# Retention and feed-forward products of a mixed pair: interleaved, or each in one go

## The chip, the cores and the metric

The kernel runs on one core of one Trainium2 chip. The metric is the device time in microseconds of one execution; a kernel's time is the median over its runs. TensorE (PE) does the matrix products, VectorE (DVE) and ScalarE (ACT) the element-wise work, GpSimd (POOL) a little on the side, and SyncE's queue (SP) issues all transfers.

## The reference

```
ret  = (q kᵀ / 8) * D          per head; D[i,j] = gamma_h^(i-j) for i >= j, else 0
x    = ret @ v                 B=4, 8 heads, 576 positions, head size 64 -> 2304 tokens x 512
xn   = x / rms(x) * rms_g
y    = (silu(xn @ w_gate) * (xn @ w_val)) @ w_out        512 -> 1536 -> 512
out  = relu(y @ w_in)^2 @ w_out2                         512 -> 2048 -> 512
```

All inputs and outputs are float32.

## The kernel before, in words

**Retention.** Two heads make a pair (128 partitions); there are 16 pairs, and pair n is written n here, pieces of it `name(n)`. The 576 positions are cut in chunks of 128 (the last of 64). Four functions do a pair: `scores(n, half)` multiplies q and k of two or three chunks into bank pair A1 (half 0) or A0 (half 1), and DVE multiplies the result with the decay mask into `ret`; `state(n)` (L256) makes four 128x64 chunk states `u` from k and v in one PSUM bank, ACT copies the first one to `R[:, 0]` and DVE makes `R[:, 1]` to `R[:, 3]` from it one after the other (L269 and L271); `outputs(n, half)` (L277) adds `R` times q and `ret` times v in a bank of tag V, and DVE writes it to X (L298). Loop pass n does scores and state of pair n and outputs of pair n-1.

**Feed-forward.** A float32 product is three products of high and low parts (`mm3`, L386 to L388). A block `pg` or `pv` is twelve matmuls of 512 columns into a bank of tag G; ACT applies silu to `pg` (L426), DVE multiplies `pv` with it (L434). Tags G and V have two banks each, handed out in turn: a tile waits until the last reader of the tile two before it in its tag is through.

**Weights.** Each weight piece is loaded raw (512 KB, L101) to one of three buffers and converted by `convert_piece`: two ACT copies (L124, L125), three DVE steps (L126, L129, L132), an ACT copy to the high part (L137), a DVE subtraction for the low part (L138). The load of a piece waits until L132 has read the buffer of the piece three before it. `halves(k)` counts half pieces and converts when there are two. `CONVERT_BEHIND` says for a phase whether a conversion is issued behind the last ACT and DVE instruction then known ("ad") or may go ahead of them ("").

**Order.** PE and SP take their instructions in the order of the code. The order on ACT, DVE and POOL is set when the kernel is built, by a planner with its own estimate of times; each engine then takes its instructions strictly in that order. Passes 1 to 7 have retention alone. From pass 8 on ("mixed") `block()` at two points of a pass puts feed-forward blocks of the first 512 tokens between the retention products: ten gate and ten value blocks at 17 points up to pass 16. `NORMS` says in which pass and half the normalization steps of 256 tokens come (squares, roots, scale, split), and `LOAD_W` where one more weight piece is loaded ahead.

Of the kernel before, what the change touches and what calls it, by code (L numbers as in the profile page):

```python
# [25 lines left out]
NPAIR = B * HP  # L26
HALF = (2 * C, S - 2 * C)
NMAX = 512
T1 = [512, 256, 512, 512, 512]
# [5 lines left out]
ORDER = [*range(NBESIDE, NF1), *range(NBESIDE)]  # L35
NWA, NWC = NGV + NKEPT // 2, 1
NWB = NF1 - NKEPT // 2 - NWC
SKIP = 1
FIRST = 7
WARM = (8, 6, 5, 5)  # L40
WARM_PAIR = {1: (1, 1), 2: (1, 1)}
NORMS = {
    (4, 0): [("squares", 0)], (4, 1): [("squares", 1)], (5, 0): [("roots", 0)], (5, 1): [("roots", 1)],
    (6, 1): [("scale", 0), ("split", 0)], (7, 0): [("scale", 1), ("split", 1)],
    (9, 1): [("squares", 2)], (11, 0): [("roots", 2)], (12, 0): [("scale", 2)],
}
LOAD_W = (3,)
CONVERT_ALONE = {2: 2, 3: 2, 7: 2}
CONVERT_BEHIND = ("", "", "ad", "ad")
RSQRT_MAGIC = float(0x5F3759DF)  # L50
# [6 lines left out]
def retention_then_glu_then_relu2(ctx: ExitStack, tc: tile.TileContext, qk, kv, w1, w2, g, cmask, cvs, cgi, cgc, cid, out):  # L57
# [15 lines left out]
    def bank(tag, name):  # L73
        return psum.tile([P, 512], F32, tag=tag, name=name)
# [30 lines left out]
    def load_ahead(i):  # L105
        while cv["load"] < min(i + cv["ahead"], cv["load_lim"]):
            load_piece()

    def convert():
        i = cv["done"]  # L110
        if i not in raws or i >= cv["lim"]:
            return False
        raw = raws.pop(i)
        with ExitStack() as behind:
            for e in CONVERT_BEHIND[cv["phase"]]:
                behind.enter_context(tc.issue_after(last_on[e].ins))
            convert_piece(i, raw)
        cv["done"] += 1
        return True
# [21 lines left out]
    def halves(k):  # L141
        cv["half"] += k
        while cv["half"] >= 2 and convert():
            cv["half"] -= 2
        cv["half"] = min(cv["half"], 2)

    def need(n):
        while cv["done"] < n:
            assert convert()
# [9 lines left out]
    alone = {"on": True}  # L159
# [13 lines left out]
    def load_kv(n):  # L173
        if n >= NPAIR:
            return
        if n > 1:
            raw_k[n] = kvp.tile([P, 4, P], F32, tag="k", name=f"k{n}")
            vsc[n] = ap.tile([P, 5, P], F32, tag="v", name=f"v{n}", bufs=4)
        else:
            t = X[:, 2 + n, :9 * P].rearrange("p (c n) -> p c n", c=9)  # L180
            raw_k[n], vsc[n] = t[:, :4], t[:, 4:]
        nc.sync.dma_start(out=raw_k[n], in_=kv[n][:, :4])
        nc.sync.dma_start(out=vsc[n], in_=kv[n][:, 4:])
# [10 lines left out]
    def keep_warm(k, new=False):  # L194
        if new:
            junk["t"] = bank("G", f"junk{len(junk)}")
        for _ in range(k):
            nc.tensor.matmul(junk["t"][:, :P], zero, zero, start=True, stop=True)
# [36 lines left out]
    def scores(n, half):  # L235
        hp = n % HP
        ps = bank2("A0" if half else "A1", f"s{n}_{half}")
        for j in range(2 + half):
            w = REM if j == 2 else C
            for h in range(2):  # L240
                score(ps[:w, h, j * C:j * C + w], n, 2 * half + j, h, w)
        t = ap.tile([P, 2, 2 * C], F32, tag="ret", name=f"ret{n}_{half}", bufs=3)
        last_on["d"] = nc.vector.tensor_tensor(
            out=t.rearrange("p h (c i) -> p h c i", c=2),
            in0=ps[:, :, :2 * C].rearrange("p h (c i) -> p h c i", c=2),
            in1=mask[:, 2 * hp:2 * hp + 2, None, :].to_broadcast([P, 2, 2, C]),
            op=ALU.mult,
        )
        rets[n, half] = t
        if half:  # L250
            last_on["d"] = nc.vector.tensor_tensor(
                out=ret4[n % 2][:REM], in0=ps[:REM, :, 2 * C:2 * C + REM],
                in1=mask[:REM, 2 * hp:2 * hp + 2, :REM], op=ALU.mult,
            )

    def state(n):  # L256
        hp = n % HP
        u = bank("G" if alone["on"] else "V", f"u{n}")
        for c in range(4):
            for h in range(2):  # L260
                r = slice(h * D, h * D + D)
                nc.tensor.matmul(
                    u[r, c * D:c * D + D], raw_k[n][:, c, r], vsc[n][:, c, r],
                    start=True, stop=True,
                )
        if n > 1:
            load_kv(n + 2)
        R = ap.tile([P, 4, D], F32, tag="R", name=f"R{n}")
        last_on["a"] = nc.scalar.activation(out=R[:, 0], in_=u[:, 0:D], func=AF.Copy)  # L269
        for c in range(1, 4):  # L270
            last_on["d"] = nc.vector.scalar_tensor_tensor(  # L271
                out=R[:, c], in0=R[:, c - 1], scalar=gc[:, hp:hp + 1], in1=u[:, c * D:c * D + D],
                op0=ALU.mult, op1=ALU.add,
            )
        Rs[n] = R

    def outputs(n, half):  # L277
        b, hp = divmod(n, HP)
        po = bank("V", f"o{n}_{half}")
        ret = rets.pop((n, half))  # L280
        chunks = ((0, C), (1, C)) if half == 0 else ((2, C), (3, C), (4, REM))
        both = [slice(h * D, h * D + D) for h in range(2)]
        for c, w in chunks:
            o = (c - 2 * half) * C
            for r in both if c else ():
                nc.tensor.matmul(
                    po[r, o:o + w], Rs[n][r, c - 1], raw_qk[n][r, 0, c * C:c * C + w],
                    start=c == max(1, 2 * half), stop=False, skip_group_check=True,
                )
        for c, w in chunks:  # L290
            o = (c - 2 * half) * C
            for h, r in enumerate(both):
                rhs = ret4[n % 2][:, h] if c == 4 else ret[:, h, o:o + w]
                nc.tensor.matmul(
                    po[r, o:o + w], vsc[n][:, c, r], rhs, start=False, stop=c == chunks[-1][0], skip_group_check=True,
                )
        t0, w = b * S + half * 2 * C, HALF[half]
        last_on["d"] = nc.vector.tensor_tensor(out=X[:, hp, t0:t0 + w], in0=po[:, :w], in1=gi[:, hp, :w], op=ALU.mult)  # L298
        if half:
            load_qk(n + 4)  # L300
# [69 lines left out]
    def split_x(tok, n, col0=0):  # L370
        for k in range(KC):
            src_, d = X[:, k, tok:tok + n], slice(col0, col0 + n)
            last_on["a"] = nc.scalar.activation(out=xh[:, k, d], in_=src_, func=AF.Copy)
            last_on["d"] = nc.vector.tensor_tensor(out=xl[:, k, d], in0=src_, in1=xh[:, k, d].bitcast(F32), op=ALU.subtract)  # L374


    off1 = [sum(T1[:i]) for i in range(len(T1))]
# [96 lines left out]

    cv["lim"] = cv["load_lim"] = NGV
    blocks = [(kind, f) for f in range(NBESIDE) for kind in (glu_gate, glu_val)]
    NPOINT = 2 * (NPAIR - FIRST) - SKIP
    points = {"n": -SKIP, "done": 0}

    def block():  # L480
        points["n"] += 1
        while points["done"] < min(len(blocks), points["n"] * len(blocks) / NPOINT):
            i = points["done"]
            need(i + 1)
            blocks[i][0](0, blocks[i][1], "G")
            points["done"] += 1
            halves(1)

    def stages(n, half):
        with tc.high_priority():  # L490
            for what, i in NORMS.get((n, half), ()):
                beside(what, i)

    for n in range(1, NPAIR + 1):
        mixed = n > FIRST
        if n in LOAD_W:
            cv["ahead"] += 1
            load_ahead(cv["done"])
        if n == FIRST + 1:
            alone["on"] = False  # L500
            cv["phase"] = 2
        if n == FIRST + 2:
            cv["phase"] = 1
        if n < NPAIR:
            scores(n, 0)
        if mixed:
            block()
        else:
            keep_warm(WARM_PAIR.get(n, (0, 0))[0], n in WARM_PAIR)
        outputs(n - 1, 0)  # L510
        stages(n, 0)
        if n < NPAIR:
            state(n)
            if n == NPAIR - 1:
                att_kv.close()
                wpool["c"] = ctx.enter_context(tc.tile_pool(name="wc", bufs=NWC, side="right", reuse_waits="tile"))
                cv["lim"] = NGV + NWC
                cv["load_lim"] = NP1
                load_ahead(cv["done"])
        if mixed:  # L520
            block()
        else:
            keep_warm(WARM_PAIR.get(n, (0, 0))[1])
        if n < NPAIR:
            scores(n, 1)
        outputs(n - 1, 1)
        stages(n, 1)
        scale_v(n + 1)
        halves(CONVERT_ALONE[n] if n in CONVERT_ALONE else 2 * mixed)
    need(NGV)  # L530
    assert points["done"] == len(blocks)
    att.close()
# [10 lines left out]
    for f in range(NBESIDE, NF1):  # L543
# [2 lines left out]
        halves(1)  # L546
        glu_val(0, f, "G")
        halves(1)
    split_x(off1[1], T1[1])
    norms = iter(())  # L550
    LAG = 2
    for f in range(NF1 + LAG):
# [161 lines left out]
```

## Time and profile before

| | us |
|---|---|
| median of 3 runs (948.32 to 952.52) | 948.55 |
| the profiled execution | 944.46 |
| its span, first to last instruction | 942.7 |
| PE busy / DVE busy / ACT busy in the span | 929.0 / 456.4 / 338.6 |
| granted TensorE clock, mean | 0.999 |

The passes with retention lie in the first 150 us of the span, the mixed ones from 48 to 150 us. PE rows are pipelined: the start of one row to the start of the next is what a matmul takes from the span, and its own duration is longer. The same holds on DVE, where a row ends some 0.08 us after the next has started. A row "x8" counts the passes of the float32 products of retention, two for each matmul of the code.

### The profile page before, as it was taken

How to read it: one execution, taken by the hardware profiler on the slowest of the kernel's cores; microseconds unless marked ns; L12 is line 12 of the kernel's file. 1: busy time of each engine (PE TensorE's matmuls, PEld its weight loads, DVE VectorE, ACT ScalarE, POOL GpSimd, SP SyncE). 2: the span in 40 equal slices, each digit the busy share in tenths (PEclk: the TensorE clock that was granted, in tenths of full speed). 3: DMA queues.
4: the chain of work that ended last, by engine and by line, in shares of the span. 5: the costliest groups of instructions: out<-in, count | busy, mean ns of one | idle time of the engine just before them, and what ended most of it. 6: DMA issues, size and time to landing. Idle time of an engine off the chain costs nothing.

```text
span 942.7 us, 12628 instructions
## 1 busy us (share of the span) xinstructions
PE 929.0 (99%) x5228; PEld 776.3 (82%) x5228; DVE 456.4 (48%) x859; ACT 338.6 (36%) x606; POOL 22.5 (2%) x56
## 2 busy tenths in 40 slices
PE   9999999999999999999999999999999999999998
PEld 8777777999888888888888888888888888888897
DVE  4987794765644123512677776442223223322322
ACT  3564552652311121112555655432223222322332
POOL 0200000021100000000000000000000000000000
PEclk9999999999999999999999999999999999999999
DMA  9865641410000000100144422001001000100010
GB/s 326 301 218 188 230 162 46 136 44 1 1 1 23 0 1 1 39 7 0 67 134 134 135 89 90 1 5 41 0 1 45 1 1 1 45 1 1 1 46 23
DMA packets 22554, 60.92 MB, mean 65 GB/s; under 512 B 2656, under 2 KB 3936, under 8 KB 22496
## 3 DMA queue, kind: packets, MB, share of 16 engines
q1 hardware_dynamic: 22496, 60.11, 18.8%
q8 instruction: 41, 0.67, 0.3%
q14 instruction: 17, 0.14, 0.0%
HBM read 55.39 MB, written 4.72 MB: 64 GB/s over the span
## 4 chain that ended last, share of the span: by engine, by line
PE 89%; DMA 5%; DVE 3%; ACT 1%; issue 1%; SPq 1%; ACTq 0%
PE pr L388 7%; PE b L628 7%; PE pr L387 7%; PE pr L386 7%; PE b L629 7%; PE b L630 7%; PE a L387 5%; PE a L386 5%; PE a L388 5%; PE pg L386 5%; PE pg L387 5%; PE pg L388 5%; PE pv L386 5%; PE pv L388 5%; PE pv L387 5%; DMA raw<-in_w 4%
## 5 line engine op out<-in xcount | busy, mean ns | idle before, releaser
L617 DVE TENSOR_TENSOR X<-X 128x512 f32<-128x512 f32 (+1 forms) x80 | 51.1, 639 | 189.3 <-ACT X L616 188.6
L415 ACT ACTIVATE h<-X 128x512 fp32r<-128x512 f32 (+1 forms) x132 | 77.5, 587 | 161.7 <-DVE X L434 86.8
L416 DVE TENSOR_TENSOR h<-X,h 128x512 fp32r<-128x512 f32 (+1 forms) x132 | 84.5, 640 | 70.7 <-ACT h L415 69.5
L388 PE MATMUL pr<-xh,w 128*128 128x512 f32 (+1 forms) x320 | 117.7, 368 | 0.0
L387 PE MATMUL pr<-xl,w 128*128 128x512 f32 (+1 forms) x320 | 117.7, 368 | 0.0
L386 PE MATMUL pr<-xh,w 128*128 128x512 f32 (+1 forms) x320 | 117.6, 368 | 0.0
L616 ACT ACTIVATE X<-pr 128x512 f32<-128x512 f32 (+1 forms) x80 | 44.5, 556 | 194.5 <-PE pr L388 194.3
L628 PE MATMUL b<-w,h 128*128 128x512 f32 x288 | 112.4, 390 | 0.0
L629 PE MATMUL b<-w,h 128*128 128x512 f32 x288 | 112.2, 390 | 0.0
L630 PE MATMUL b<-w,h 128*128 128x512 f32 x288 | 112.0, 389 | 0.0
L386 PE MATMUL pv<-xh,w 128*128 128x512 f32 (+1 forms) x240 | 90.5, 377 | 0.0
L387 PE MATMUL pg<-xl,w 128*128 128x512 f32 (+1 forms) x240 | 88.6, 369 | 1.6 <-DVE xl L374 1.6
L386 PE MATMUL pg<-xh,w 128*128 128x512 f32 (+1 forms) x240 | 89.6, 373 | 0.0
L387 PE MATMUL a<-h,w 128*128 128x512 f32 (+1 forms) x240 | 88.5, 369 | 0.0
L386 PE MATMUL a<-h,w 128*128 128x512 f32 (+1 forms) x240 | 88.5, 369 | 0.0
L388 PE MATMUL pv<-xh,w 128*128 128x512 f32 (+1 forms) x240 | 88.4, 368 | 0.0
L388 PE MATMUL pg<-xh,w 128*128 128x512 f32 (+1 forms) x240 | 88.4, 368 | 0.0
L388 PE MATMUL a<-h,w 128*128 128x512 f32 (+1 forms) x240 | 88.4, 368 | 0.0
L387 PE MATMUL pv<-xl,w 128*128 128x512 f32 (+1 forms) x240 | 88.3, 368 | 0.0
L434 DVE TENSOR_TENSOR X<-pv,X 128x512 f32<-128x512 f32 (+1 forms) x52 | 32.7, 628 | 110.9 <-PE pv L388 109.1
L426 ACT ACTIVATE X<-pg 128x512 f32<-128x512 f32 (+1 forms) x52 | 28.5, 549 | 114.0 <-PE pg L388 114.0
L387 PEld LDWEIGHTS pr<-xl,w 128*128 128x128 f32 x320 | 60.3, 188 | 10.7
(93 smaller groups left out, 1412.0 us busy)
## 6 DMA issues: line engine op xcount, KB each, us to landing
raw<-in_w SPq DMA_DIRECT2D x68, 512.0 KB, 3.7
X<-in_qk SPq DMA_DIRECT2D x11, 576.0 KB, 6.2
out<-o SPq DMA_DIRECT2D x18, 256.0 KB, 2.1
v<-in_kv SPq DMA_DIRECT2D x14, 320.0 KB, 4.3
k<-in_kv SPq DMA_DIRECT2D x14, 256.0 KB, 3.1
qk<-in_qk SPq DMA_DIRECT2D x4, 576.0 KB, 4.2
X<-in_kv SPq DMA_DIRECT2D x2, 320.0 KB, 5.3
X<-in_kv SPq DMA_DIRECT2D x2, 256.0 KB, 5.0
```

Source lines behind the costliest of these rows:

```text
L386: nc.tensor.matmul(dst, whi, xhi, start=start, stop=False, skip_group_check=True)
L387: nc.tensor.matmul(dst, whi, xlo, start=False, stop=False, skip_group_check=True)
L388: nc.tensor.matmul(dst, wlo, xhi, start=False, stop=stop, skip_group_check=True)
L415: last_on["a"] = nc.scalar.activation(out=h[:, 0, :n], in_=s, func=AF.Copy)
L416: last_on["d"] = nc.vector.tensor_tensor(out=h[:, 1, :n], in0=s, in1=h[:, 0, :n].bitcast(F32), op=ALU.subtract)
L426: last_on["a"] = nc.scalar.activation(out=s, in_=pg[:, :n], func=AF.Silu)
L434: last_on["d"] = nc.vector.tensor_tensor(out=s, in0=pv[:, :n], in1=s, op=ALU.mult)
L616: last_on["a"] = nc.scalar.activation(out=s, in_=pg[:, :n], func=AF.Relu)
L617: last_on["d"] = nc.vector.tensor_tensor(out=s, in0=s, in1=s, op=ALU.mult)
L628: nc.tensor.matmul(a[m], hh, w[:, 0], start=f == 0, stop=False)
L629: nc.tensor.matmul(a[m], hh, w[:, 1], start=False, stop=False)
L630: nc.tensor.matmul(a[m], hl, w[:, 0], start=False, stop=f == NF2 - 1)
```

## The change

From pass 8 to 15 all retention products of a pass come one behind the other, and behind them the feed-forward blocks in one go: two or three blocks in each of eight passes instead of one or two at each of 17 points. Pass 16 has retention products only. `state` takes its bank from tag G in all passes. In `NORMS` the roots of the third 256 tokens move from (11, 0) to (11, 1) and their scale from (12, 0) to (13, 0). The third weight piece loaded ahead is asked for in pass 4 instead of 3, and phase 2 of the conversions ("ad") begins in pass 7 instead of 8. `split_x` behind the mixed stretch gets high priority.

```diff
-SKIP = 1
-    (9, 1): [("squares", 2)], (11, 0): [("roots", 2)], (12, 0): [("scale", 2)],
+    (9, 1): [("squares", 2)], (11, 1): [("roots", 2)], (13, 0): [("scale", 2)],
-LOAD_W = (3,)
+LOAD_W = (4,)
     def state(n):
         hp = n % HP
-        u = bank("G" if alone["on"] else "V", f"u{n}")
+        u = bank("G", f"u{n}")
-    NPOINT = 2 * (NPAIR - FIRST) - SKIP
-    points = {"n": -SKIP, "done": 0}
-    def block():
+    NPOINT = NPAIR - FIRST - 1
+    points = {"n": 0, "done": 0}
+    def some_blocks():
         points["n"] += 1
-        while points["done"] < min(len(blocks), points["n"] * len(blocks) / NPOINT):
+        while points["done"] + 1 <= points["n"] * len(blocks) / NPOINT:
...
         if n == FIRST + 1:
             alone["on"] = False
+        if n == FIRST:
             cv["phase"] = 2
...
             scores(n, 0)
-        if mixed:
-            block()
-        else:
-            keep_warm(WARM_PAIR.get(n, (0, 0))[0], n in WARM_PAIR)
+        keep_warm(WARM_PAIR.get(n, (0, 0))[0], n in WARM_PAIR)
         outputs(n - 1, 0)
         stages(n, 0)
...
-        if mixed:
-            block()
-        else:
-            keep_warm(WARM_PAIR.get(n, (0, 0))[1])
+        keep_warm(WARM_PAIR.get(n, (0, 0))[1])
         if n < NPAIR:
             scores(n, 1)
         outputs(n - 1, 1)
...
         halves(CONVERT_ALONE[n] if n in CONVERT_ALONE else 2 * mixed)
+        if mixed and n < NPAIR:
+            some_blocks()
+            halves(1)
...
-    split_x(off1[1], T1[1])
+    with tc.high_priority():
+        split_x(off1[1], T1[1])
```

In the lists below the number in a name such as `s_1_751` only tells tiles apart: `s_h` is half h of scores, `o_h` of outputs, `u` a bank of states, and behind `pg_` and `pv_` stands the block. Line numbers of the kernel after are one lower.

**PE, pass 8**, before, from the scores of pair 8 (`s_0_718`) to the first block. `R_674` are the states of pair 7, `u_733` the chunk states of pair 8:

```order
L233 MATMUL s_0_718<-X 128x128 x4
L286 MATMUL o_0_725<-X,R_674 64x128 x2
L294 MATMUL o_0_725<-ret_0_636,v_504 64x128 x4
L262 MATMUL u_733<-v_581,k_580 64x64 x8
L386 MATMUL pg_0_751<-xh,w_318 128x512
L387 MATMUL pg_0_751<-xl,w_318 128x512
```

And after, the same stretch:

```order
L232 MATMUL s_0_718<-X 128x128 x4
L285 MATMUL o_0_725<-X,R_674 64x128 x2
L293 MATMUL o_0_725<-ret_0_636,v_504 64x128 x4
L261 MATMUL u_733<-v_581,k_580 64x64 x8
L232 MATMUL s_1_751<-X 128x128 x4
L232 MATMUL s_1_751<-X 64x64 x2
L285 MATMUL o_1_761<-X,R_674 64x128 x4
L285 MATMUL o_1_761<-X,R_674 64x64 x2
L293 MATMUL o_1_761<-ret_1_686,v_504 64x128 x4
L293 MATMUL o_1_761<-ret_1_95,v_504 64x64 x2
L385 MATMUL pg_0_790<-xh,w_318 128x512
```

The second halves of scores and outputs moved from behind blocks 0 of gate and value to ahead of them.

**DVE, pass 8**, before, from the second step of `R_674` to the states of pair 8 (`R_746`):

```order
L271 SCALAR_TENSOR_TENSOR R_674<-R_674,gc,u_661 128x64
L243 TENSOR_TENSOR ret_0_723<-s_0_718,mask 128x512
L298 TENSOR_TENSOR X<-o_0_725,gi 128x256
L271 SCALAR_TENSOR_TENSOR R_674<-R_674,gc,u_661 128x64
L271 SCALAR_TENSOR_TENSOR R_746<-R_746,gc,u_733 128x64
L129 SCALAR_TENSOR_TENSOR raw_713<-raw_713 128x512
L271 SCALAR_TENSOR_TENSOR R_746<-R_746,gc,u_733 128x64 x2
```

And after, from the conversion of the third weight piece (`u_707`, `raw_316`) to the third step of `R_674`:

```order
L125 TENSOR_SCALAR u_707<-u_707 128x512
L128 SCALAR_TENSOR_TENSOR raw_316<-raw_316 128x512
L270 SCALAR_TENSOR_TENSOR R_674<-R_674,gc,u_661 128x64
L242 TENSOR_TENSOR ret_0_723<-s_0_718,mask 128x512
L297 TENSOR_TENSOR X<-o_0_725,gi 128x256
L270 SCALAR_TENSOR_TENSOR R_746<-R_746,gc,u_733 128x64
L242 TENSOR_TENSOR ret_1_758<-s_1_751,mask 128x512
L250 TENSOR_TENSOR ret_0_94<-s_1_751,mask 64x128
L131 SCALAR_TENSOR_TENSOR u_707<-u_707,raw_316 128x512
L270 SCALAR_TENSOR_TENSOR R_674<-R_674,gc,u_661 128x64
```

The conversion of that piece moved here from between the pairs 4 and 5, and the third step of `R_674` now stands behind it and behind the masks of `s_1_751`.

**DVE, around the value block 7** (`pv_7`), before; `R_1488` are the states made from `u_1479`:

```order
L271 SCALAR_TENSOR_TENSOR R_1488<-R_1488,gc,u_1479 128x64
L434 TENSOR_TENSOR X<-pv_7_1493,X 128x512
L126 TENSOR_SCALAR u_1734<-u_1734 128x512
L129 SCALAR_TENSOR_TENSOR raw_1657<-raw_1657 128x512
L243 TENSOR_TENSOR ret_1_1525<-s_1_1518,mask 128x512
L251 TENSOR_TENSOR ret_0_94<-s_1_1518,mask 64x128
L132 SCALAR_TENSOR_TENSOR u_1723<-u_1723,raw_1622 128x512
L271 SCALAR_TENSOR_TENSOR R_1488<-R_1488,gc,u_1479 128x64
```

And after, in pass 14, with `u_1512` and `R_1521`:

```order
L297 TENSOR_TENSOR X<-o_1_1536,gi 128x320
L131 SCALAR_TENSOR_TENSOR u_1709<-u_1709,raw_1583 128x512
L270 SCALAR_TENSOR_TENSOR R_1521<-R_1521,gc,u_1512 128x64
L131 SCALAR_TENSOR_TENSOR u_1734<-u_1734,raw_1644 128x512
L433 TENSOR_TENSOR X<-pv_7_1563,X 128x512
L270 SCALAR_TENSOR_TENSOR R_1521<-R_1521,gc,u_1512 128x64
L137 TENSOR_TENSOR w_1717<-u_1709,w_1717 128x512
```

In both, the last step of the states stands behind the product of `pv_7`; the tile that takes the bank of `u` is an `o_0` of tag V before and the next block, `pg_8`, of tag G after.

## Rows read from the trace of the kernel before

**Rows 1.** Waits of PE: us in total, times, longest us:

```profile
PE u L262 <- DVE X L298: 3.8, 3, 2.0
PE ssq L356 <- DVE aside L352: 2.1, 1, 2.1
PE pg L387 <- DVE xl L374: 1.6, 2, 1.2
PE o L286 <- DVE R L271: 1.3, 1, 1.3
```

**Rows 2.** Busy time by engine, sum over the mixed stretch, 48.33 to 150.14 us:

```profile
sum 101.81, PE 96.67 PEld 75.38 DVE 81.49 ACT 52.19 POOL 2.32; mean PE 13.81 PEld 10.77 DVE 11.64 ACT 7.46 POOL 0.33
```

**Rows 3.** PE in order of time: start us, us, engine, line, operation:

```profile
22.38 0.72 PE L233 MATMUL s<-X 64*128 64x128 f32 x8
...
24.44 0.92 PE L233 MATMUL s<-X 64*128 64x128 f32 x10
...
26.59 0.71 PE L233 MATMUL s<-X 64*128 64x128 f32 x8
...
112.30 0.50 PE L386 MATMUL pg<-xh,w 128*128 128x512 f32 x1
...
115.24 0.92 PE L233 MATMUL s<-X 64*128 64x128 f32 x10
...
153.01 0.39 PE L386 MATMUL pv<-xh,w 128*128 128x512 f32 x1
...
155.73 0.39 PE L386 MATMUL pg<-xh,w 128*128 128x512 f32 x1
```

**Rows 4.** DVE in order of time, three rows of conversions:

```profile
58.11 0.42 DVE L126 TENSOR_SCALAR u<-u 128x512 f32<-128x512 f32 x1
58.44 0.68 DVE L129 SCALAR_TENSOR_TENSOR raw<-raw 128x512 int32<-128x512 int32 x1
59.04 0.42 DVE L126 TENSOR_SCALAR u<-u 128x512 f32<-128x512 f32 x1
```

**Rows 5.** DVE in order of time, passes 7 and 8:

```profile
43.43 1.66 DVE L326 SCALAR_TENSOR_TENSOR X<-X,gsb,rms 128x256 f32<-128x256 f32 x4
...
51.58 0.27 DVE L271 SCALAR_TENSOR_TENSOR R<-R,gc,u 128x64 f32<-128x64 f32 x1
51.77 0.68 DVE L243 TENSOR_TENSOR ret<-s,mask 128x512 f32<-128x512 f32 x1
```

**Rows 6.** PE in order of time, pass 8:

```profile
51.04 0.69 PE L262 MATMUL u<-v,k 128*64 128x64 f32 x16 [1.04 <-DVE X L298]
51.65 0.50 PE L386 MATMUL pg<-xh,w 128*128 128x512 f32 x1
```

**Rows 7.** Waits of DVE, 48 to 150 us, and of SP's queue, 0 to 170 us:

```profile
DVE u L126 <- ACT u L124: 4.6, 6, 1.3
DVE raw L129 <- ACT raw L125: 1.9, 2, 1.5
...
SPq L101 <- DVE u L132: 61.6, 14, 17.9
```

**Rows 8.** Loads of weight pieces, 60 to 145 us, from issue to landing:

```profile
DMA to landing us min/median/max: 3.3/4.7/5.8
```

**Rows 9.** ACT's second copy of a conversion, 43 to 151 us: busy, mean ns of one, idle before:

```profile
L125 ACT ACTIVATE raw<-raw 128x512 int32<-128x512 uint32 x21 | 14.1, 671 | 4.8 <-DMA raw<-in_w 4.8
```

**Rows 10.** Loads of v, 44 to 145 us, from issue to landing:

```profile
DMA to landing us min/median/max: 3.1/4.1/4.6
```

**Rows 11.** DVE's product of the value block 4, whose last matmul starts at 98.8 us:

```profile
99.21 0.69 DVE L434 TENSOR_TENSOR kept<-pv,kept 128x512 f32<-128x512 f32 x1 [1.17 <-PE pv L388]
```

**Rows 12.** PE at the end of the value block 7, and DVE's product of it:

```profile
128.09 0.92 PE L233 MATMUL s<-qk 64*128 64x128 f32 x10
...
131.04 0.68 DVE L434 TENSOR_TENSOR X<-pv,X 128x512 f32<-128x512 f32 x1
```

**Rows 13.** Busy time of 2 us in which PE waits, and the granted clock:

```profile
88.00:90.00 2.00, 0.22 (x6) 0.23 (x8) 2.00 (x6) 0.00 (x0) 0.00 (x0) 1.00 0.02 4
```

## The prediction

> **What bounds the kernel now.** I read the busy times first: PE is busy 929 of 942.7 us, at full clock. So time can come only from what PE waits for, or from products that start later than they could. The waits of PE come next [rows 1]: 8.8 us in the rows shown, all on DVE. Three waits are of `u` (1.04, 2.01 and 0.77 us, 3.8 together), one of `o` (1.3); these four, 5.1 us, lie in the mixed stretch, where `u` shares the two banks of tag V with the outputs. The wait of `ssq` (2.1) lies ahead of it, that of `pg` on `xl` (1.6) behind it. The sum over the mixed stretch shows what the second engine is: DVE is busy 81.5 of 101.8 us [rows 2], four fifths, and it takes its rows strictly in order. What the new order asks of DVE, and when, decides.
>
> **What goes.** (1) The switch between small retention products and blocks. A lone block takes 112.30 to 115.24, 2.94 us; one between two others 153.01 to 155.73, 2.72 [rows 3]. A pair of retention alone takes 22.38 to 26.59, 4.21 us [rows 3], and the pieces of a mixed pair add up to the same, so a burst of blocks costs 0.22 us once. Before there are 17 bursts (17 points with at least one block), after 8: 9 x 0.22 = 2.0 us less. Nothing hides this, it is PE's own time; half and all of it are its bounds.
> (2) The four waits in the mixed stretch, 5.1 us [rows 1]: they hang on tag V's banks, which `u` no longer takes. I take all as gone, and count below what is late next.
> (3) The wait of `ssq`, 2.1 us. DVE's queue ahead of it loses one conversion's first three steps, 0.33 + 0.60 + 0.60 [rows 4] = 1.5 us. Of these only the first stands ahead of the output on which the squares wait; behind that, ACT's square takes about as long as the other two. I take 1.1; bounds 0 and 2.1.
>
> **What is late next.** DVE's costs are from start to start: a full 512-column step 0.60, a one-input conversion step 0.33 [rows 4], a step of R 0.19 [rows 5].
>
> *Pass 8.* DVE starts the first scale at 43.43 and is through its scales, splits and masks at 51.58 without a pause [rows 5], and 8.15 us of the same rows stand there after. Then the new order has 0.33 + 0.60 of the conversion, R 0.19, mask 0.60, output 0.33, R 0.19, masks 0.60 + 0.20, the conversion's third step 0.60, and then the third step of R for pair 7, with its own end 0.27: 51.58 + 3.91 = 55.5. The last chunk of `o_1` reads that step. PE without waits would have `u` at 50.0 (51.04 less its wait [rows 6]), 0.6 later `s_1`, 2.15 for the halves (24.44 to 26.59), and the first block at 52.75 [rows 3, 6]. With R at 55.6, and the 0.8 us of output products behind it, the block starts at 56.4: 3.7 us of waiting. Behind it stand all blocks. Before, R was wanted two blocks later, and only the 1.04 in (2) was paid. Bounds 3.0 and 4.3: the rows are the same, only ACT's copies in between could shift.
>
> *Passes 9 and 10.* The states now lie in a bank of tag G, so the second block behind `u` waits for all three steps of R. Count from the end of `pv_0`: PE needs two retention bursts (4.3 each), four blocks up to `pg_3` (2.72) and two switches to get to `pg_3`, 20.0 us. DVE has 45 rows from the product of `pv_0` to the third step of R of pass 10: 26 at 0.60, 9 at 0.34, 2 at 0.40, 8 at 0.20: 21.1. That alone is 1.1 late. In it are three conversion steps that wait for a load. A load waits for L132 of the piece three before (61.6 us of SP's waits [rows 7]), lands 3.3 to 5.8 us after issue, median 4.7 [rows 8], and needs 0.7 on ACT [rows 9]; the tightest place in the order leaves six DVE rows, 3.3 us, for it, so each costs DVE some 1.3, and three loads now follow a pair's k, v and q in one go. The whole would be 1.1 + 3 x 1.3, 5 us of waiting. Before, 21 conversions cost DVE 6.5 us in such waits [rows 7], 0.3 each; seven pieces at that price would make it 3. I take 4; bounds 1 and 5.5.
>
> *Pass 12.* The first of its pieces is issued when `o_1` of pass 11 has freed q's buffer (SP's queue is in order), and converted from 5.8 us after that; 23 DVE rows to the third step of R take 10.9. PE gets to `pv_5` in 16.1 (ssq, three blocks, retention, one block). 16.7 and some 0.6 of pauses against 16.1: 1.2 taken, bounds 0 and 2.
>
> *Pass 13.* ACT scales v behind the load that `u` releases: issue 0.5, landing 4.1 (3.1 to 4.6) [rows 10], scale 1.0, a high part 0.55, DVE's low part and R 0.9: 7.0 after `u`. PE is at `pv_6` 2.15 + 2.83, 5.0 after it: 2.0 late, 1.0 if the load lands at the lower end, as one that is alone on the queues may: 1.5 taken, bounds 0.3 and 2.2.
>
> *Pass 14.* The third step of R stands behind the product of `pv_7`, and the next block, `pg_8`, wants the bank. At best DVE takes `pv_7` at once, as it does block 4 [rows 11]: then 0.2 + 0.6 + 0.3, 1.2 us with the signal. Before, it took that very product at 131.04, when PE had left the block at 128.09 [rows 12], 3.0 late, which makes 3.9. The same order stood there before, but only `o_0` wanted it, six microseconds later, and even that is the wait of 1.3 [rows 1]. I take 3.0; bounds 1.2 and 3.9.
>
> Passes 11 and 15 have R well ahead of the second block: nothing. The split behind the mixed stretch: in the new order two of its four DVE rows stand behind a block's product, two conversion steps and a low part, so the wait for `xl` moves from the second product to the third: 0.3 worse; bounds 1.6 better (all gone) and 0.8 worse.
>
> **Sum.** 3.7 + 4.0 + 1.2 + 1.5 + 3.0 = 13.4 in place of 5.1: +8.3. Less 2.0 for switches and 1.1 for `ssq`, plus 0.3: +5.5 us. The profiled execution took 944.46, which makes 950.0; the timed runs' median lies 4.1 above it (948.55), so the median should come to 954.0. With all lower bounds: 5.5 - 5.1 - 2.0 - 2.1 - 1.6 = -5.3, 943.3; with all upper ones 17.9 - 5.1 - 1.0 + 0.8 = +12.6, 961.
>
> **Rivals.** *The vector queue keeps pace* (948.5). Its rows need 21.1 of PE's 20.0 us in passes 9 and 10, and if PE's waits give it time and loads land at the lower end (3.3), the new waits are 8 us, and +2.9 - 3.1 + 0.3 is nothing. For it: DVE is a fifth idle [rows 2]. Against: that idle time is waiting for loads and for PE.
> *Faster: the third step of R comes before the pair's second block in all passes but 8 and 14.* One mechanism: a bank of tag G is held by `u` for the second halves and one block, 5.1 us; as long as DVE is less than 2 us behind PE, nobody waits for it. Then 3.7 + 1.2 = 4.9 replaces 5.1, and -0.2 - 2.0 - 2.1 with the split's gain of 0.4 is -4.7: 943.8 and below. DVE's lag at the ends of value blocks decides: 0.1 at block 4 [rows 11] speaks for it, 3.0 at block 7 [rows 12] against.
> *Loads pile up.* Three loads in one go behind 1.1 MB of k, v and q: all load waits at their upper ends, +9 to +12: 959.
> *The clock falls.* In the two microseconds in which PE stood still before, the granted clock stayed 1.00 [rows 13]; no row shows the lower level. In pass 8 PE now stands longer, with a few small products in between. If it fell to 1.2 GHz, each 2.72 us block behind it could take up to twice as long: two blocks, +5.4 on the forecast, 959.
> The Trainium skill ("TensorE: Matmul & The Clock Gate", HAM oscillation) says that idle gaps of TensorE beyond some length send its clock to the lower level, and that this is paid at every gap. By that rule the long new wait could cost the clock and the forecast would be the last rival's; the trace, with 1.00 through its longest waits, does not decide it.
>
> **How the numbers follow.** Forecast 0.50, vector queue keeps pace 0.25, faster 0.10, loads pile up 0.12, clock 0.03. About 0.5%, 4.7 us, is what can be told from no change: 943.8 to 953.3. Of the forecast three fifths lie beyond it (0.30) and two fifths within (0.20). Slower 0.30 + 0.12 + 0.03 = 0.45, within 0.20 + 0.25 = 0.45, faster 0.10. The range leaves out half of the faster and half of the pile-up case: 944 to 959; the forecast's own is 951 to 956.5.
>
> **What would show it.** PE waits at `o_1` of pass 8 on DVE's R, 3 to 4 us in up to three pieces, and at `pg_3` and `pg_8` on R (L270), together over 5 us. No wait of `u` on an output. `ssq` waits about 1.0. A burst of two blocks takes 5.66 us. DVE's own waits on ACT's `u` grow beyond 6.5 us. I am wrong if the waits on R together stay under 8 us, if the wait in pass 8 is missing (then the tiles of R are not what `o_1` waits for), or if the mixed stretch (first scores of pair 8 to `pg_10`) is shorter than 101.8 us.

## The result and the profile after

The kernel after takes 962.62 us (median of 4 runs, 959.99 to 963.08) beside 948.43 us for the kernel before: ratio 1.0135, 95% interval 1.0106 to 1.0164. It is 1.35% slower. 954.0 was predicted, with a range of 944 to 959: the direction was right, the size was not.

| | before | after |
|---|---|---|
| the profiled execution, us | 944.46 | 962.54 |
| its span | 942.7 | 960.8 |
| PE busy / DVE busy / ACT busy | 929.0 / 456.4 / 338.6 | 935.0 / 459.1 / 338.4 |
| granted clock, mean | 0.999 | 0.989 |
| first scores of pair 8 to the first row of `pg_10` | 101.8 | 117.5 |

The waits of PE after, from 20 to 175 us, in the columns of [rows 1]:

```profile
PE pg L385 <- DVE X L433: 4.5, 1, 4.5
PE pv L385 <- DVE R L270: 4.5, 3, 2.7
PE o L285 <- DVE R L270: 2.7, 2, 2.0
PE pg L385 <- ACT w L136: 2.1, 1, 2.1
PE s L232 <- DVE ret L250: 1.6, 1, 1.6
PE o L285 <- DVE X L297: 1.3, 2, 1.0
PE ssq L355 <- DVE aside L351: 0.9, 1, 0.9
PE u L261 <- PE ssq L355: 0.3, 1, 0.3
```

No `u` waits for an output any more, as foreseen; but the first six rows, all in the mixed stretch, add up to 16.7 us where 5.1 stood [rows 1]. The sum over that stretch, 49.50 to 166.97 us, against [rows 2]:

```profile
sum 117.47, PE 100.80 PEld 79.30 DVE 87.85 ACT 55.61 POOL 2.34; mean PE 100.80 PEld 79.30 DVE 87.85 ACT 55.61 POOL 2.34
```

The stretch is 15.7 us longer, and DVE is idle for 29.6 us of it, 20.3 before [rows 2]: it does not run out of time, it is late at certain places. PE is busy 4.1 us longer with fewer switches, which waits do not explain. Windows of 2 us behind the waits of pass 8 and of pass 14 do (engines as in [rows 13]; the number behind POOL's is the granted clock):

```profile
56.00:58.00 2.00, 0.38 (x4) 0.00 (x0) 2.00 (x6) 0.00 (x0) 0.00 (x0) 0.50 0.00 0
58.00:60.00 2.00, 1.60 (x16) 1.44 (x16) 1.51 (x5) 0.63 (x1) 0.00 (x0) 0.50 0.38 70
60.00:62.00 2.00, 2.00 (x9) 1.55 (x6) 1.78 (x4) 0.00 (x0) 0.00 (x0) 0.50 1.00 372
...
148.00:150.00 2.00, 2.00 (x6) 1.54 (x6) 0.30 (x1) 0.00 (x0) 0.00 (x0) 0.50 0.97 371
```

0.50 is the lower level, 1.2 GHz. An estimate of what it took is PE's busy time multiplied by (1 - clock), summed over such windows of the whole span: 8.6 us after (1.6 in the front, 5.4 in the mixed stretch, 1.6 behind it), nothing in the profiled execution of before. So the 18.1 us of span are 9.5 us at full clock and 8.6 us of clock. What is left of each kernel's span without this loss is called "at full clock" below; two profiled executions of the kernel before came to 942.7 and 943.4 by it, so differences under 1 us tell nothing.

### The profile page after: what moved, and what is told of

The parts are those of the page before. It is cut to its first block, busy times and chain, and to the rows that moved or that the text cites. A ratio compares the mean times of both kernels' runs of the same rounds, so it can differ in the third digit from the quotient of the medians.

```text
span 960.8 us, 12631 instructions
## 1 busy us (share of the span) xinstructions
PE 935.0 (97%) x5228; PEld 782.1 (81%) x5228; DVE 459.1 (48%) x859; ACT 338.4 (35%) x606; POOL 22.1 (2%) x56
## 4 chain that ended last, share of the span: by engine, by line
PE 88%; DVE 5%; DMA 4%; ACT 2%; issue 1%; SPq 0%; ACTq 0%
PE b L626 7%; PE pr L385 7%; PE pr L387 7%; PE pr L386 7%; PE b L627 7%; PE b L628 7%; PE a L386 5%; PE a L385 5%; PE a L387 5%; PE pg L385 5%; PE pg L386 5%; PE pg L387 5%; PE pv L385 5%; PE pv L387 5%; PE pv L386 5%; DMA raw<-in_w 2%
## 5 line engine op out<-in xcount | busy, mean ns | idle before, releaser
L385 PE MATMUL pg<-xh,w 128*128 128x512 f32 (+1 forms) x240 | 91.2, 380 | 6.5 <-DVE X L433 4.5
L387 PE MATMUL pg<-xh,w 128*128 128x512 f32 (+1 forms) x240 | 89.8, 374 | 0.0
L433 DVE TENSOR_TENSOR X<-pv,X 128x512 f32<-128x512 f32 (+1 forms) x52 | 32.6, 628 | 114.7 <-PE pv L387 114.4
```

The source lines that it names most:

```text
L385: nc.tensor.matmul(dst, whi, xhi, start=start, stop=False, skip_group_check=True)
L387: nc.tensor.matmul(dst, wlo, xhi, start=False, stop=stop, skip_group_check=True)
L433: last_on["d"] = nc.vector.tensor_tensor(out=s, in0=pv[:, :n], in1=s, op=ALU.mult)
```

## The experiments

Ratios are to runs of the kernel before on the same chip, with 95% intervals; the clock is the mean over the runs, "lost" and "full clock" are of the profiled execution.

| run | median | ratio | clock | span | lost | full clock |
|---|---|---|---|---|---|---|
| before | 948.4 to 950.0 | | 0.994 | 942.7 | 0.0 | 942.7 |
| after | 962.62 | 1.0135 [1.0106, 1.0164] | 0.988 | 960.8 | 8.6 | 952.2 |
| e1 weight undone | 962.66 | 1.0145 [1.0113, 1.0176] | 0.988 | 961.3 | 11.3 | 950.0 |
| e2 bank undone | 964.11 | 1.0169 [1.0146, 1.0192] | 0.985 | 960.2 | 12.1 | 948.1 |
| e10 grouping alone | 961.26 | 1.0129 [1.0091, 1.0167] | 0.989 | 962.1 | 10.2 | 951.9 |
| e3 bank alone | 949.35 | 1.0023 [0.9999, 1.0047] | 0.994 | 949.0 | 6.7 | 942.3 |
| e11 weight alone | 950.41 | 1.0015 [0.9994, 1.0036] | 0.994 | 948.5 | 6.8 | 941.7 |
| e4 after, states first | 950.21 | 1.0019 [1.0001, 1.0037] | 0.994 | 953.4 | 8.2 | 945.2 |
| e12 the same, bank V | 950.39 | 1.0019 [1.0002, 1.0036] | 0.995 | 949.0 | 1.6 | 947.4 |
| e8 before, bank G, states first | 953.27 | 1.0025 [1.0003, 1.0047] | 0.994 | 952.6 | 5.1 | 947.5 |
| e15 after, behind | 952.00 | 1.0024 [0.9999, 1.0048] | 0.992 | 952.0 | 8.1 | 943.9 |
| e16 before, behind | 964.30 | 1.0148 [1.0111, 1.0186] | 0.989 | 962.7 | 9.5 | 953.2 |
| e13 after, no loads | 965.79 | 1.0155 [1.0133, 1.0178] | 0.988 | 963.6 | 9.1 | 954.5 |
| e14 before, no loads | 946.60 | 0.9986 [0.9964, 1.0008] | 0.995 | 942.4 | 1.7 | 940.7 |
| e5 before again | 956.06 (1 run) | | 0.987 | 954.3 | 10.9 | 943.4 |
| e6 before, fill | 951.68 | 1.0031 [1.0012, 1.0051] | 0.993 | 951.5 | 6.6 | 944.9 |
| e9 before, fill in ssq's bank | 948.00 | 1.0002 [0.9987, 1.0016] | 0.997 | 945.2 | 1.7 | 943.5 |
| e7 after, fill | 963.32 | 1.0141 [1.0111, 1.0170] | 0.992 | 963.5 | 8.1 | 955.4 |

### Which part of the change it is

e1 takes the weight part back:

```diff
-LOAD_W = (4,)
+LOAD_W = (3,)
-        if n == FIRST:
             cv["phase"] = 2
```

> The kernel after, but the weight part undone: the third piece is asked for in pass 3 and phase 2 of the conversions begins in pass 8, as before. DVE's order then has the third step of R for pair 7 ahead of the second halves' masks, with no conversion ahead of it. Theory A (late steps of R: everything that DVE has ahead of the third step of R is what TensorE waits for, and each long wait costs granted clock too): pass 8's waits fall from 4.67 us to 1 to 2, the clock of 54 to 62 us stays 1.00 (2.5 us more), the waits of pv_1, pv_5 and pg_8 stay: 956, between 953 and 958. Theory B (the weight part is the cause of the loss): 950 or less. Theory C (the grouping itself lumps the work of DVE and of the loads, whatever stands ahead of R): 960 or more, the waits only move.

e2 takes the bank back, `u = bank("G" if alone["on"] else "V", f"u{n}")`:

> The kernel after, but the states of a mixed pass in tag V as before. Theory A: the waits of pv_1, pv_5, pv_6 and pg_8 on R (2.68, 1.57, 0.20, 4.48: 8.9 us) go, with the clock's fall behind pg_8 (1.7 us), pass 8 stays as it is: 952, between 950 and 955. Theory C: the blocks wait for the products or the weights instead, less than 4 us come back: 958 or more. If the bank were everything (theory D): 949 or less.

e10 does both, so that the grouping of the products remains, with the moved norm steps and the priority of the split:

> The kernel after with bank and weight part both undone: the grouping of the products (with the moved norm steps and the split's priority) alone. The parts undone one at a time left 2.2 us (weight) and 4.1 us (bank) less at full clock, and nothing in the median. Theory A: both together, 946 at full clock, and with a clock like that of before (0.994) 950 to 952; with the clock of after (0.987) 955 to 957. Theory C (the grouping itself makes DVE late): 958 or more.

e3 is the kernel before with `u = bank("G", f"u{n}")` and nothing else, e11 the kernel before with the weight part and nothing else:

> The kernel before, with only the bank changed: states in tag G in all passes. Theory A: the three waits of u on an output (3.8 us) go, and since one block at most follows u before the second halves, the block that wants the bank comes 6 us later: 946, between 944 and 949. Theory D (the bank alone makes the loss): 954 or more, with waits of blocks on R of 6 us and more together.

> The kernel before with the weight part alone (third piece asked for in pass 4, phase 2 from pass 7). Theory A: the wait of ssq falls from 2.1 to 1.2 us with that of u behind it, the third step of R for pair 7 stands behind one more conversion, but o_1 wants it two blocks later: 947 to 949.5. Theory B (this part is what loses): 955 or more.

Theories B and D fall: each part alone costs nothing that can be told (e3, e11), and taking both away leaves the whole loss (e10). Theory A's arithmetic falls too. At full clock e1 and e2 gained 2.2 and 4.1 us and gave them back to the clock; both together gained 0.3. The waits moved. With the states in tag V, the waits of PE in e10 from 48 to 168 us are these:

```profile
PE o L285 <- DVE X L297: 8.3, 6, 3.0
PE u L261 <- DVE X L297: 5.6, 2, 4.5
PE ssq L355 <- DVE X L297: 2.7, 1, 2.7
```

16.6 us again, now for outputs in place of `R`: which tile waits is the bank's choice, that something waits is not. Theory C, that grouping makes DVE late, is the one that holds. The moved norm steps and the split's priority were not undone alone. The steps come in passes 11 and 13, and 9.4 of the 16.7 us of waits after lie ahead of them, in passes 8 to 10; e4 and e15 below keep both parts and are without the loss.

### What DVE is late with

e4 leaves DVE's work as it is and moves it: from pass 7 to 15 conversions, and products of value blocks, are issued behind the third step of R of the newest pair.

```diff
+            if cv["rf"]:
+                behind.enter_context(tc.issue_after(last_on["r"].ins))
             convert_piece(i, raw)
...
-            last_on["d"] = nc.vector.scalar_tensor_tensor(
+            last_on["r"] = last_on["d"] = nc.vector.scalar_tensor_tensor(
...
+        cv["rf"] = FIRST - 1 < n < NPAIR
```

> The kernel after, but from pass 7 to 15 each conversion and each block's product is issued behind the third step of R of the newest pair, so DVE's order has R ahead of them. Theory A: the waits on R (o_1 of pass 8, pv_1, pv_5, pg_8: 12 us) fall under 3, the granted clock stays 1.00 in the mixed stretch: 948, between 944 and 953. Theory C: the conversions are late instead, and blocks wait for w by as much: 957 or more.

It took 950.2 us: the loss is gone, and the mean clock is that of before, though the profiled execution had falls in the mixed stretch (0.54 at 102 to 104 us, 0.50 at 154 to 156). The four largest waits of PE that remain from 48 to 168 us:

```profile
PE pv L387 <- DVE kept L438: 2.6, 1, 2.6
PE pv L387 <- DVE X L438: 2.0, 1, 2.0
PE pg L387 <- DVE R L272: 1.4, 1, 1.4
PE u L263 <- DVE kept L438: 1.3, 1, 1.3
```

R, 7.2 us after, is down to 2.2 (1.4 and 0.8 of `o`); part of it came back as waits for products. e12 (the same in tag V) and e8 (the kernel before, states in G, conversions behind R) ask whether more is to be had (for e4 at full clock the table's 945.2 holds, not the 943.2 of the first expectation):

> The kernel after with R ahead of conversions and products, and the states in tag V. With the states first (in tag G) blocks still waited 4.6 us for a product and 2.2 us for R, 943.2 at full clock. If the bank's turn is what binds them there: these waits go, 939 to 941 at full clock, median 944 to 947, faster than both kernels. If DVE is late as a whole, u and o wait for outputs instead, as with the bank alone undone: 949 to 953.

> The kernel before, with the states in tag G, and conversions of passes 7 to 15 issued behind the third step of R of the newest pair. Theory A: with the bank alone, u no longer waits (3.8 less), but blocks waited for R (2.9) and a silu (2.2); with R ahead of the conversions these go too: waits of 4 to 5 us in all (ssq 2.1, xl 1.6), 938 to 940 without the clock's loss, median 943 to 946. Theory C (conversions are late then): waits of blocks on w of 3 us and more, 948 or more.

It is not. In e12 `u` and `o` wait for outputs in the mixed stretch (3.4 and 4.1 us), as its second answer says. In e8 `pg` waits for R for 2.8 us and others for silu and weights: interleaved products do not gain from states first.

That led to the last pair: one edit, in both kernels. Phase 2 of the conversions ("ad", behind the last ACT and DVE instruction known) lasts through all mixed passes:

```diff
-        if n == FIRST + 2:
-            cv["phase"] = 1
```

> The kernel after with one edit: phase 2 of the conversions lasts through all mixed passes, so each conversion is issued behind the last ACT and DVE instruction then known, that is behind all retention steps of its pass, masks and outputs as well as R. Removing the loads left the loss in place (965.8), putting R alone first took it away (950.2). If the place of the conversions on DVE is the cause: the loss is gone here too, 945 to 951, with TensorE's waits on R in the mixed stretch under 3 us. If the number of DVE's rows were the cause, order would not help: 957 or more (blocks wait for their weights).

> The kernel before with the same edit, as the other half of the comparison. Retention's steps come first here too: u waits less for outputs (3.8 before), o less for R (1.3): 945 to 948 if conversions are still in time; if blocks wait for their weights, since a conversion now starts later, 949 to 952. With e15 it tells what the grouping is worth when DVE takes retention first: level with or up to 2 us under this run.

| median, us | conversions may go ahead | conversions behind |
|---|---|---|
| interleaved products | 948.4 (before) | 964.3 (e16) |
| grouped products | 962.6 (after) | 952.0 (e15) |

Not all four ran side by side: against before on the same chip e16 is at 1.0148, after at 1.0135 and e15 at 1.0024. So neither grouping nor the place of the conversions is good or bad by itself. Both expectations missed in part. e15 took 1 us more than the 945 to 951 foreseen, and PE's waits for R did not fall under 3 us (7.0 remain); it is the others from 48 to 168 us that went, from 9.5 to 0.9. e16 was foreseen at 952 at most and took 964.3. Its blocks wait for weights (first and last of these rows, 20 to 175 us):

```profile
PE pg L386 <- ACT w L137: 9.3, 4, 3.9
PE u L262 <- DVE X L298: 3.1, 3, 1.3
PE ssq L356 <- DVE aside L352: 2.1, 1, 2.1
PE pg L388 <- DVE w L138: 2.1, 3, 1.1
```

The reading that fits all four, argued from durations: retention's own DVE rows of one pair take 0.60 + 0.33 + 3 x 0.19 + 0.60 + 0.20 + 0.40 = 2.7 us, and a grouped pair takes PE 4.2 [rows 3]. There is no room in it for a conversion (0.33 + 3 x 0.60 = 2.1) unless PE waits; between two halves with a block of 2.9 us there is. DVE in pass 14 of the kernel after (in order of time) is an example, from the first step of R to the third, with the first row of `pg_8` on PE behind it:

```profile
142.51 0.27 DVE L270 SCALAR_TENSOR_TENSOR R<-R,gc,u 128x64 f32<-128x64 f32 x1
142.71 0.68 DVE L242 TENSOR_TENSOR ret<-s,mask 128x512 f32<-128x512 f32 x1
...
143.51 0.67 DVE L128 SCALAR_TENSOR_TENSOR raw<-raw 128x512 int32<-128x512 int32 x1
144.10 0.41 DVE L125 TENSOR_SCALAR u<-u 128x512 f32<-128x512 f32 x1
144.44 0.67 DVE L137 TENSOR_TENSOR w<-u,w 128x512 fp32r<-128x512 f32 x1
145.04 0.47 DVE L297 TENSOR_TENSOR X<-o,gi 128x320 f32<-128x320 f32 x1
145.44 0.67 DVE L131 SCALAR_TENSOR_TENSOR u<-u,raw 128x512 int32<-128x512 int32 x1
146.04 0.26 DVE L270 SCALAR_TENSOR_TENSOR R<-R,gc,u 128x64 f32<-128x64 f32 x1
146.24 0.67 DVE L131 SCALAR_TENSOR_TENSOR u<-u,raw 128x512 int32<-128x512 int32 x1
146.84 0.67 DVE L433 TENSOR_TENSOR X<-pv,X 128x512 f32<-128x512 f32 x1
147.44 0.26 DVE L270 SCALAR_TENSOR_TENSOR R<-R,gc,u 128x64 f32<-128x64 f32 x1
```

```profile
147.56 0.80 PE L385 MATMUL pg<-xh,w 128*128 128x512 f32 x1 [4.48 <-DVE X L433]
```

Not one idle gap, and five conversion steps (L128, L125, L137, L131, L131: 2.7 us from start to start) between the first step of R and the product of `pv_7` (L433), for which `pg_8` waited 4.48 us. It did not wait for the third step: that ended at 147.70, when `pg_8` was running. So the bank that `pg_8` took here was that of `pv_7` and not, as banks handed out strictly in turn would give, that of `u`. In e1 and e13 `pg_8` starts in the same way behind the product and ahead of the end of R (waits of 4.92 and 3.80 us).

### Whether it is the loads

DVE's waits after, 48 to 168 us, had grown as foreseen, against [rows 7]:

```profile
DVE u L125 <- ACT u L123: 11.1, 6, 3.0
...
DVE raw L128 <- ACT raw L124: 1.4, 2, 0.9
```

These are waits for loads, passed on by ACT. e13 and e14 fill the buffers of pieces 3 to 19 on GpSimd in place of `nc.sync.dma_start`:

```diff
+        if 3 <= i < 2 * NBESIDE:
+            nc.gpsimd.memset(t.rearrange("p n t -> p (n t)").bitcast(F32), 1.0)
+        else:
```

> The kernel after, with weight pieces 3 to 19 (those of the blocks in the mixed passes) not loaded: GpSimd fills their buffer with a constant instead, as soon as it is free, and the conversion works on that. So a conversion waits 1 to 2 us for its data instead of 3.3 to 5.8. If late loads in front of DVE's in-order queue are the cause: DVE's wait on ACT's first copy in the mixed stretch falls from 11.1 us (after) to under 4, TensorE's waits there from 16.7 to under 7, and the time to 946 to 951. If DVE is late by the number of its rows alone: 957 or more.

> The kernel before with the same pieces not loaded. DVE waited 4.6 us for ACT's first copies in its mixed stretch; if these are what made u and o wait (5.1), 943 to 947; if not, 948 as before. Against it stands the same kernel with the products grouped: if the loads are the whole loss of grouping, that one is level with this or up to 2 us faster (fewer switches).

With the grouping the loss stayed (965.8, 954.5 at full clock), though DVE's wait for ACT's first copies fell from 11.1 to 6.9 us. That is more than the 4 expected, but 4.7 of it are at pieces from 20 on, which were still loaded; at the filled ones 2.2 remain. Late loads of these pieces are not needed for the loss. That they add nothing in the kernel after is not shown: the planner, which knows the fill to be quick, put the rows in another order. Without the grouping nothing that can be told was won.

### The clock

In e3 the front is the same as in the kernel before, and so is its wait of `ssq`. PE around it, in e3:

```profile
34.74 0.61 PE L356 MATMUL ssq<-ones,aside 128*128 128x1 f32 x4 [2.10 <-DVE aside L352]
...
36.71 1.15 PE L286 MATMUL o<-X,R 64*64 64x128 f32 x11
...
45.82 0.38 PE L363 MATMUL rms<-aside 128*128 128x128 f32 x1
```

and in the kernel before:

```profile
34.62 0.61 PE L356 MATMUL ssq<-ones,aside 128*128 128x1 f32 x4 [2.10 <-DVE aside L352]
...
36.58 0.71 PE L286 MATMUL o<-X,R 64*64 64x128 f32 x11
...
42.68 0.49 PE L363 MATMUL rms<-aside 128*128 128x128 f32 x2
```

The same wait of 2.10 us, and in one execution the products behind it stretch (0.71 to 1.15) and `rms` comes 3.1 us later, in the other nothing happens. So the kernel before was profiled again, unchanged (e5), and the wait filled with seven products whose result nobody reads (e6, e9); e7 fills four waits of the kernel after.

> The kernel before, unchanged, profiled a second time. Its first profiled execution had a granted clock of 1.00 throughout and took 944.5, 4.1 us under the median of its runs; with the bank alone changed, the clock fell to 0.50 behind the same wait of ssq (2.10 us, at 34.7) and the passes behind it took 3.1 us longer. Theory E (whether the clock falls behind a wait of about 2 us is chance, execution by execution, and the median of before holds one or two such falls): this execution has at least one fall and takes 946 to 952, and its span without the clock's loss is 942 to 943.5. Rival: no fall and 944 to 946; then the 4.1 us come from something else. One execution can't tell much if it has none.

> The kernel before, with seven products of the mask with itself (results not used, into unused columns of the first scores' bank) ahead of the first ssq, so that TensorE works through the wait of 2.1 us instead of standing still. Theory E: the fall behind that wait is gone in all executions; if it is the commonest one, 946 to 947.5, with a smaller spread. Rival (idle time is not what lowers the clock): 948.4 as before. If the products delay the work behind them: 949.

> The kernel before, again with seven products of the mask with itself ahead of the first ssq, now into unused columns of ssq's own bank, which is free by then (in the first attempt they waited themselves, for a mask step of DVE). Theory E (TensorE's standing still behind 32.5 us is what lowers the clock at 35 to 48): no fall in this stretch, and the executions with the lowest clock (0.988, spans of 951) become rare: mean clock 0.996 or more instead of 0.994, median 1 to 2.5 us under before. Rival (falls there come whatever TensorE does): clock 0.994 and the time of before.

> The kernel after, with such products in four of its waits: 3 ahead of the first ssq, 10 ahead of the last chunk products of o_1 in pass 8, 7 ahead of pg_3, 15 ahead of pg_8. Nothing waits less; theory E: the falls at 36, 56, 94 and 148 us (6.6 us of lost clock) do not come, and the time is 955 to 957. Theory A without the clock (waits are everything): 961 to 963. If the new order on DVE that they bring moves waits elsewhere, the trace shows them.

e5: 956.06 us, above the 946 to 952 expected, with falls at 34 to 50, 96 to 104 and 174 to 180 us; 10.9 us lost, and 943.4 at full clock, as in the first execution (942.7). Beyond this one, 97 executions of before beside these runs have a span and a mean clock each: two at a clock of 0.999 have spans of 943.2 and 943.7, 17 at 0.994 a median of 947.2, two at 0.988 951.6; a straight fit has 0.75 us for each 0.001, correlation -0.92. Most of the spread of this kernel goes with the clock. The four runs after had 0.987 to 0.989: at 0.988 before and after stand at 951.6 and 960.8, 9.2 us apart, close to the 9.5 at full clock.

e6 and e7 missed their aim: their products went to a bank that a mask step was still reading, so they waited themselves (`s` for `ret`, 2.7 us in e6) and added to the time. They decide nothing. In e9 they went to ssq's own bank. PE and the granted clock there:

```profile
34.13 1.83 PE L356 MATMUL ssq<-mask 128*128 128x128 f32 x14
36.31 0.61 PE L358 MATMUL ssq<-ones,aside 128*128 128x1 f32 x4 [0.34 <-DVE aside L352]
```

```profile
36.00:40.00 4.00, 3.69 (x60) 3.36 (x60) 3.93 (x11) 2.54 (x5) 0.68 (x4) 1.00 0.50 163
40.00:44.00 4.00, 4.00 (x68) 3.44 (x70) 2.42 (x10) 1.12 (x3) 2.85 (x16) 1.00 0.70 226
```

No fall there, and the mean clock over 12 runs is 0.997, lowest 0.994; the 29 runs of before on that chip have 0.995, and seven of them are under 0.994. By the slope above the difference is worth some 1.4 us; 0.6 is seen in the medians (948.0 beside 948.6), not to be told from none. The Trainium skill ("TensorE: Matmul & The Clock Gate", HAM oscillation) has it that idle gaps of TensorE beyond some length bring the lower level, and that its kernel paid at every gap. That gaps bring it these runs bear out; paid at every gap it was not: the gap of 2.10 us was paid in e3 and e5 and not in the first profile of before, and in the kernel after the clock fell behind a wait of 2.06 us (`pg_3`) and not behind one of 2.68 (`pv_1`).

## Why the prediction was too low

Right were the sign and most of the places: pass 8 waits at `o_1`, no `u` waits for an output, `ssq` waits 0.9 (1.0 foreseen), a burst of two blocks takes 5.66 us (76.53 to 82.19), DVE's load waits are beyond 6.5. But one sign of being wrong came up as well: the waits on R together are 7.2 us, under the 8 that the prediction asks for, because `pg_3` and `pg_8` were released by something else. The terms:

| term | foreseen | measured |
|---|---|---|
| pass 8 | 3.7 (3.0 to 4.3) | 1.62 + 0.34 + 0.69 + 2.02 = 4.67 |
| passes 9 and 10 | 4.0 (1 to 5.5) | 2.68 + 2.06 = 4.74 |
| pass 12 | 1.2 (0 to 2) | 1.57 |
| pass 13 | 1.5 (0.3 to 2.2) | 1.01 + 0.20 = 1.21 |
| pass 14 | 3.0 (1.2 to 3.9) | 4.48 |
| sum | 13.4 | 16.67 |

Two terms of the sum failed, the waits by 3.3 us and the clock by 4.6, and the mechanism held only in part.

1. Waits, 3.3 us too low, in two terms above all. Pass 8: "8.15 us of the same rows stand there after" was wrong. DVE waited 1.60 us for ACT inside them, since on ACT a scale of v that waited 4.25 us for its load and the two copies of the moved conversion stood ahead:

```profile
46.33 1.01 ACT L225 ACTIVATE v<-v,vs 128x320 f32<-128x320 f32 x2 [4.25 <-DMA v<-in_kv]
47.25 0.64 ACT L123 ACTIVATE u<-raw 128x512 f32<-128x512 f32 x1
47.80 0.65 ACT L124 ACTIVATE raw<-raw 128x512 int32<-128x512 uint32 x1
48.35 1.32 ACT L372 ACTIVATE xh<-X 128x256 fp32r<-128x256 f32 x4
```

```profile
48.79 0.42 DVE L373 TENSOR_TENSOR xl<-X,xh 128x256 fp32r<-128x256 f32 x1 [1.60 <-ACT xh L372]
```

Pass 14 was over its upper bound, and its step was wrong: `pg_8` was to wait for the third step of R in the bank of `u`, but it waited for the product of `pv_7`. DVE began that product at 146.84, 3.8 us after the end of PE's last row (142.69 + 0.39), behind the five conversion steps shown above. Two smaller places came out near their numbers by other ways. In pass 10 `pg_3` was released by its weights (ACT done at 91.40), 0.08 us behind the third step of R (91.32). In pass 13 only 0.20 is the wait foreseen, `pv_6` on R; the 1.01 is `o_1` on the output of `o_0`, which the sum had at nothing.

```profile
90.77 0.63 ACT L136 ACTIVATE w<-u 128x512 fp32r<-128x512 f32 x1 [1.82 <-DVE u L131]
91.06 0.26 DVE L270 SCALAR_TENSOR_TENSOR R<-R,gc,u 128x64 f32<-128x64 f32 x1
91.47 0.47 PE L385 MATMUL pg<-xh,w 128*128 128x512 f32 x1 [2.06 <-ACT w L136]
```

The 5.5 us foreseen and these 3.3 make 8.8 at full clock; 9.5 was measured. The switches gave less than the 2.0 foreseen: without the 5.4 of clock PE is busy 95.4 us in the mixed stretch, 1.3 under the 96.67 of [rows 2].

2. The clock, 4.6 us. "The timed runs' median lies 4.1 above it" was carried over as if it were a constant. It is the clock that the usual execution of before loses and the profiled one by chance did not; after, the loss is 8.6. The rival "The clock falls" got 0.03 because no row of that one trace showed the lower level. That its price, 5.4, is also what the mixed stretch lost is luck: it stands for two blocks behind pass 8, and the trace has three falls, 2.2 us behind pass 8, 1.7 behind `pg_3` and 1.5 behind `pg_8`. 4.0 us at full clock (9.5 less 5.5) and 4.6 of clock are the 8.6 us between 954.0 and 962.6. Either alone would have stayed inside the range (958.0, 958.6).

3. The mechanism was too narrow. The states' bank was taken for the door through which DVE's lateness reaches PE; with the bank in V (e10) it came in through the outputs. The rival "faster" asked for R ahead of the second block: e4 made that so, and the time is then level with before, not 4.7 under it, since blocks wait for products in its place. What the four runs with conversions ahead and behind show instead is that DVE's order as a whole has to fit the grouping.

What stays open: why the gap of `ssq` lowers the clock in one execution and not in another, how much of DVE's lateness after is loads, and whether the durations above are the whole reason why the two orders of products want opposite orders on DVE.

## What to carry to other kernels

When matmuls are regrouped, an in-order vector queue has to be regrouped with them: the same conversions were right ahead of retention in one order of the products (948.4 against 964.3) and right behind it in the other (952.0 against 962.6). The bank and the prefetch moved alongside only chose here which tile showed the wait. And look at the granted clock of several executions before taking the profiled one for the median: here 11.6 us of added waits came with 4.6 us more of lost clock than the usual execution of before has.

## What was not expected of the hardware

The same 2.10 us of standing still lost no clock in the first profile of the kernel before and some 6.5 us in the second (e5, 34 to 50 us), and 97 executions of that kernel have spans from 942.8 to 952.8 us, most of which goes with the clock. A fall is long against the gap: in e5 the clock was at 0.50 from 36 to 48 us behind one wait of 2.1:

```profile
36.00:40.00 4.00, 4.00 (x43) 3.52 (x45) 3.12 (x11) 1.54 (x4) 2.18 (x9) 0.50 0.58 203
44.00:48.00 4.00, 4.00 (x47) 3.66 (x46) 1.89 (x6) 0.22 (x1) 1.31 (x7) 0.50 0.29 91
```

With seven small products in the gap (e9) the profiled execution had 1.00 there.
